# Sparse attention with a mixture of depths: transposes by 64-row halves, and a new order of the step

## The chip, the cores and the metric

The kernel runs on one core of a Trainium2 chip. A core has five engines that work side by side, each through its own queue in order: TensorE (matmuls, and transposes through it), VectorE, ScalarE, GpSimd and SyncE, which only issues DMAs here. They wait for each other through semaphores. The metric is the time of the device in microseconds for one execution, lower is better; three executions were timed. Cores and dies play no part, since there is only one core.

## The reference

Two blocks, one behind the other. Batch 8, 8 heads, 576 tokens, head size 64, all float32.

```python
scores = scale * np.matmul(q, k.transpose(0, 1, 3, 2))          # 8 x 8 x 576 x 576
kth = np.partition(scores, -top_k, axis=-1)[..., -top_k:-top_k + 1]   # top_k = 32
scores = np.where(scores >= kth, scores, -1e9)
attn = softmax(scores)
x = heads side by side of np.matmul(attn, v)                     # 8 x 576 x 512

for b in range(B):                                               # mixture of depths
    s = x[b] @ w_gate                                            # one gate for each token
    top = the 128 tokens of b with the largest gate
    h = np.maximum(x[b, top] @ w1, 0)                            # 512 -> 1024
    out[b] = x[b]
    out[b, top] += sigmoid(s[top])[:, None] * (h @ w2)           # 1024 -> 512
```

In each row of the scores only the 32 largest count. Finding the 32nd largest of each of 36,864 rows is the work that has no matmul in it.

## The kernel before, in words

**Units.** The work on the attention is cut into units of 128 query rows by two heads (the last 64 queries of a batch entry go as 64 rows by four heads). A batch entry has 18 units (4, 4, 4, 4 and 2), the kernel has N = 144. The list `units` holds them in order.

**Steps.** One long loop, `for n in range(-1, N)`, is a software pipeline written out by hand. In step n the engines work on six units at once:

- unit n + 1: TensorE multiplies queries by keys (`multiply`, into the four PSUM banks `ps`), ScalarE copies the scores to SBUF (`keep`, tile `sc`, of which there are five);
- unit n: VectorE searches the scores for a bound (`bound_of`): 14 instructions take the 8 largest of a seventh of a row for each of two heads (`cand`), then three rounds of maxima and replacements merge them (`best`, `bound`);
- unit n - 1: ScalarE takes the sign of bound minus score and counts it (`part`, tile `sides`, one instruction a head), GpSimd multiplies scores by signs (`y`, one product a head), so that what lies above the bound turns negative, and fills eight more places of `y` from the counts (`fill`);
- unit n - 2: VectorE takes the 8 largest of each row of `y` (`kth_of`, tile `next`); the last is the 32nd largest score;
- unit n - 3: the mask `less` of scores below the 32nd, in bfloat16, by ScalarE for the first head and by GpSimd for the second (`mask_of`);
- unit n - 4: TensorE turns the scores (`turn` for 4 chunks of each of two heads into the two banks `ptr`, `turn_last` for the rest of 64 + 64 columns into `av`), and on top of each transposed chunk it adds mask times -2^90 times the identity. ScalarE takes the exponential (`pT`, `last`), TensorE multiplies by the values into `av` (`values`), ScalarE copies the result (`xs`). The exponential of what is masked is 0; the sum of the weights comes from a column of ones beside the values.

**What rides along.** When a tile of 128 queries has all its heads, VectorE takes a reciprocal (`rden`) in the next step and GpSimd divides (`x`); one step later VectorE takes the dot product with the gate's weights (`prod`, in `dot`). It is placed in the middle of the search for candidates (`amid_late`), so it is queued between two of its instructions. When a batch entry is complete, its mixture of depths runs as a generator, `mixture`, of which the steps listed in `mix_at` call one piece each: counts of larger gates, a gather of 128 rows (an indirect DMA of GpSimd), four transposes (`xe_ps`), eight pieces of four matmuls (`h_ps`), eight matmuls (`y_ps`), a scatter that adds. In the step after a piece, `flush()` lets ScalarE copy what it left in PSUM. Keys and queries of the next batch entry are loaded by SyncE and turned in pieces (`loads`): TensorE puts up to two transposes into free columns of the scores' banks, and ScalarE copies them to `kT` or `qT`.

**What sets the order.** Every engine's instructions are kept in the order in which the program names them (`InOrder`, whose line 45 is therefore the line of nearly all instructions in the profile). So the order of calls in the loop is each engine's queue. In a step after the first ones, TensorE has: turn, last block, transposes of the loads, scores, values, the mixture's piece. ScalarE has: `pT`, `last`, `less`, copies left by the mixture in the step before, copies of the loads, `sc`, `xs`, and the two `sides`. GpSimd has: `less`, small work, two `y`, `fill`. VectorE has: candidates and merges for the bound, small work, two `next`. The first four steps have smaller banks and an order of their own. After step N - 1 an ending, written out, finishes the last units (`weigh_unit`, `values_unit`), the gates, and the mixtures of the last two batch entries.

Of the kernel before, what the change touches and what calls it, by code (L numbers as in the profile page):

```python
# [10 lines left out]
AF = mybir.ActivationFunctionType  # L11
ALU = mybir.AluOpType
FP32 = mybir.dt.float32
BF16 = mybir.dt.bfloat16
# [17 lines left out]
J = 4  # L32
# [16 lines left out]
def kernel(  # L49
# [12 lines left out]
    P = nc.NUM_PARTITIONS  # L62
# [4 lines left out]
    NT = J + 1  # L67
# [133 lines left out]
        )  # L201

    late, vector_late, pool_late = [], [], []
    amid_late = []

    kept, values_bank = [], [None]

    after_kth = []

    def flush():  # L210
        while late:
            late.pop(0)()

# [23 lines left out]
    class Rows:  # L237
# [370 lines left out]
    def turn_some(tr, z, less):  # L608

        pe.transpose(tr, z, ident)  # L610
        if less is not None:
            pe.matmul(
                tr, less, out_of_reach, start=False, stop=True, skip_group_check=True
            )

    def room_to_turn():
        return ps_tr.tile([P, 2, J, P], FP32, name="ptr"), ps_av.tile(
            [P, 512], FP32, name="av"
        )

    def turn(z, tr, less=None):

        for i in range(2):
            for c in range(J):
                at = slice(c * P + i * R, (c + 1) * P + i * R)
                turn_some(
                    tr[:, i, c, :], z[:, i, at], None if less is None else less[:, i, at]
                )

    def turn_last(z, av, less=None):  # L630

# [10 lines left out]
    def values(t, g, pT, last, av, vs):  # L642

        vt, vpair = vs  # L650
        for i, heads in enumerate(heads_of(t, g)):
            for c in range(J):
                for r in (0, R):
                    h = heads[-1 if r else 0][0]
                    pe.matmul(
                        av[r : r + R, i * DE : (i + 1) * DE],
                        pT[:, i, c, r : r + R],
                        vt[:, h, c, :],
                        start=(c == 0 and i == 0),
                        stop=False,  # L660
                        skip_group_check=True,
                    )
# [75 lines left out]
    def mixture(row0, pg, rank, exact=False):  # L738
# [116 lines left out]
        late.append(  # L855
            lambda ps=ps: act.copy(out=xeT, in_=ps.rearrange("p (c i) -> p c i", c=NDC))
        )
        hT = modpool.tile([P, NFC, CAP], FP32, name="hT")
        for fc in range(NFC):
            yield  # L860
            if fc == 1:
                vector_late.append(squash)
            if fc % 2 == 0:
                ps = ps_misc.tile([P, 2, CAP], FP32, name="h_ps", tag="misc")
            multiply_h(ps[:, fc % 2, :], fc, xeT)
            if fc % 2 == 1:
                late.append(
                    lambda ps=ps, fc=fc: act.activation(
                        hT[:, fc - 1 : fc + 1, :], ps, AF.Relu
                    )  # L870
                )

        for fc in range(NFC):
# [7 lines left out]
        late.append(  # L881
            lambda ps=ps: act.activation(gy, ps, AF.Copy, scale=g)
        )
        pool_late.append(lambda: add_rows(gy, row_i))

    def multiply_places(ps, pick, pg):

# [46 lines left out]
    def add_rows(gy, row_i):  # L934

        put_rows(gy, row_i, compute_op=ALU.add)
# [87 lines left out]
    for b in range(B - 1):  # L1024
        n = (b + 1) * per_batch + mix_at_of.get(b, mix_at)[6]
        mix_steps[n].remove(b)
        place_steps[n] = b
    mixtures = {}
    qkv = {0: room_for_qkv(0)}

# [15 lines left out]
    inverting = normalised = None  # L1046
    of_batch = {}
    scs, bounds, ys, next8s, masks = {}, {}, {}, {}, {}

    def is_unit(n):  # L1050
        return 0 <= n < N

    def weigh(sc, tr, av, less):

        turn(sc, tr, less)
        tr_last = turn_last(sc, av, less)
        pT = ptpool.tile([P, 2, J, P], FP32, name="pT")
        last = ptpool.tile([P, P], FP32, name="last")

        def exp():  # L1060
            act.activation(pT, tr, AF.Exp, scale=scale)
            act.activation(last, tr_last, AF.Exp, scale=scale)

        return pT, last, exp

    def bound_of(n):
        b, i = divmod(n, per_batch)
# [2 lines left out]
        find_bound(scs[n], bounds[b][:, i, :, :])  # L1070

    def what_is_below(n):
        at, sc = 2 * n, scs[n]
        b, i = divmod(n, per_batch)
        bound = bounds[b][:, i, :, :]
        sides = wkpool.tile([P, 2, S], BF16, name="sides")
        y = wkpool.tile([P, 2, S + 8], FP32, name="y")
        for i in range(2):
            part(i, sc, bound, at, sides)
            pool.tensor_tensor(y[:, i, 0:S], sc[:, i, :], sides[:, i, :], ALU.mult)  # L1080
        fill(y, at)
        ys[n] = y

    def kth_of(n):
# [23 lines left out]
    for n in range(-1, N):  # L1108
# [40 lines left out]

        if is_unit(n - 4):  # L1150
            tr, av = room_to_turn()
            pT, last, exp = weigh(scs.pop(n - 4), tr, av, masks.pop(n - 4))
            exp()
        if is_unit(n - 3):
            mask_of(n - 3, (act, None) if n in scatter_steps else None)
        flush()
        if is_unit(n + 1):
            b, t, g = units[n + 1]
            kT, qT = qkv[b][0:2]
            b, i = divmod(n, per_batch)  # L1160
            if n + 1 < NHP:
                ps = room_for_first_scores()
                multiply(t, g, kT, qT, ps)
                if is_unit(n - 1):
                    what_is_below(n - 1)
                stay_busy((10, 10, 20, 30)[n + 1])
            else:
                ps = room_for_scores()
                loads = list(islice(loading, first_loads[i] if b == 0 else loads_at[i]))
                halves = [ps[:, a, :, HALF : HALF + P] for a in range(2)]  # L1170
                for load, half in zip(loads, halves):
                    load[0](half)
                multiply(t, g, kT, qT, by_head(ps))
                for load, half in zip(loads, halves):
                    load[1](half)
                if n == NHP - 1:
                    stay_busy(20)
            scs[n + 1] = keep(ps)
        if is_unit(n - 4):
            b4, t4, g4 = units[n - 4]  # L1180
            values(t4, g4, pT, last, av, qkv[b4][2])
            if n in place_steps:
                values_bank[0] = av
                next(mixtures[place_steps[n]])
            if g4 == 0:
# [21 lines left out]
            after_kth.pop(0)()  # L1207


        if is_unit(n - 1) and n + 1 >= NHP:  # L1210
            what_is_below(n - 1)

        if gating is not None:
            b, t = gating
            if t == J:
                store(out[b], of_batch[b][0])
                mixtures[b] = mixture(float(b * S), of_batch[b][1], ranks[:, b, :])
        for b in mix_steps.get(n, ()):
# [21 lines left out]

    def weigh_unit(m):
        tr, av = other_room(m) if (N - m) % 2 else room_to_turn()
        weighed[m] = *weigh(scs.pop(m), tr, av, masks.pop(m)), av

    def values_unit(m):
        pT, last, _, av = weighed[m]
# [371 lines left out]
```

## Time and profile before

| | |
|---|---|
| median of three runs | 814.96 us (814.26 to 816.5) |
| the profiled execution | 816.28 us, of it the span of the profile 814.4 us |
| TensorE matmuls | 777.2 us busy, 10231 instructions |
| VectorE | 783.5 us busy, 4655 instructions |
| ScalarE | 729.5 us busy, 1577 instructions |
| GpSimd | 721.6 us busy, 722 instructions |
| DMA | 50.38 MB, mean 62 GB/s |
| TensorE's granted clock | 0.998 |

How to read it: the span is the time from the first to the last instruction in the trace, and the profiled execution takes 1.9 us more than its span. Busy is the time in which an engine has an instruction in work, waiting not included. A matmul's end is modelled and matmuls overlap each other, so TensorE's busy time says little; for it, the distance from one start to the next is the useful number. The same holds in a smaller way for VectorE and ScalarE: an instruction of `cand` lasts 0.227 us, but the next begins after 0.145 us.

Almost all is steady work. The first 40 us hold the loading of the first keys and queries, with VectorE 32.5 us busy. From 40 to 770 us a step takes 4.7 us at first and about 5.3 us on average once a mixture runs beside it; a batch entry takes 95.88 us (the exponential `pT` begins at 384.24 in one and at 480.12 in the same step of the next). The last 45 us are the ending, in which VectorE is 22.6 us busy.

The largest groups of the page's list of instructions:

```profile
L45 POOL TENSOR_TENSOR y<-sc,sides 128x576 f32<-128x576 f32 x288 | 365.8, 1294 | 51.0 <-ACT sides L45 49.3
L45 DVE MAX8 cand<-sc 128x8 f32<-128x82 f32 (+1 forms) x2016 | 314.0, 227 | 4.3 <-ACT sc L45 4.2
L45 POOL TENSOR_SCALAR less<-sc,next 128x576 bf16<-128x576 f32 x135 | 233.2, 1728 | 2.2 <-DVE next L45 1.2
L45 ACT ACTIVATE sides<-sc,bound 128x576 bf16<-128x576 f32 x288 | 223.5, 791 | 0.0
L45 PE MATMUL ptr<-out_of_reach,less 128*128 128x128 bf16 x1136 | 203.3, 219 | 18.0 <-POOL less L45 17.1
L45 PE MATMUL ptr<-ident,sc 128*128 128x128 f32 x1136 | 214.6, 280 | 0.0
L45 DVE MAX8 next<-y 128x8 f32<-128x584 f32 x288 | 204.4, 751 | 0.5 <-POOL y L45 0.5
L45 ACT ACTIVATE pT<-ptr 128x1024 f32<-128x1024 f32 x142 | 145.3, 1024 | 39.5 <-PE ptr L45 38.5
```

Each line gives engine and operation, tile written and tiles read, shapes, count, then busy us and mean ns of one, and last the idle time before them with what ended it. PE is TensorE, DVE VectorE, ACT ScalarE, POOL GpSimd, SP SyncE.

### The profile page before, as it was taken

The page shows a single profiled execution, that of the slowest core. Times are in us where ns is not written, and L with a number is a line of the kernel's source. Part 1 is how long each engine was busy: PE and PEld are TensorE (multiplying, and loading weights), DVE is VectorE, ACT ScalarE, POOL GpSimd, SP SyncE. Part 2 cuts the span into 40 slices and gives each one's busy share as a digit, 9 for nine tenths or more (in the row PEclk, how much of TensorE's full clock was granted, in tenths as well). Part 3 has the DMA queues.
Part 4 walks back from the last instruction along what each step waited for, and adds up shares of the span by engine and source line. Part 5 has one row for each costly group of instructions (what it writes and reads, how often), then busy time and mean ns, then how long its engine had stood idle before and what let it go on. Part 6 is the DMA issues. An engine that isn't in the chain of part 4 may idle for free. (4 is left out here: it accounts for less than half of the span.)

```text
span 814.4 us, 28453 instructions
## 1 busy us (share of the span) xinstructions
PE 777.2 (95%) x10231; PEld 600.3 (74%) x10231; DVE 783.5 (96%) x4655; ACT 729.5 (90%) x1577; POOL 721.6 (89%) x722
## 2 busy tenths in 40 slices
PE   8988888888999999999999999999999999999987
PEld 6766666667887778877787777877788777867756
DVE  6999999999999999999999999999999999999962
ACT  5999999999999999999999999999999999879840
POOL 3899999999999999999999999999999999998921
PEclk9999999999999999999999999999999999999999
DMA  8931214121151123221251221512224102001021
GB/s 169 287 89 28 52 58 106 29 53 28 60 114 26 43 59 90 66 54 33 74 106 29 54 41 60 100 28 54 41 80 94 28 3 79 23 5 25 2 72 30
DMA packets 121732, 50.38 MB, mean 62 GB/s; under 512 B 116016, under 2 KB 116016, under 8 KB 120560
## 3 DMA queue, kind: packets, MB, share of 16 engines
q1 hardware_dynamic: 118368, 43.94, 22.0%
q0 software_dynamic: 1744, 4.20, 2.9%
q8 instruction: 82, 1.34, 0.7%
q14 instruction: 66, 0.54, 0.2%
q10 hardware_dynamic: 1472, 0.36, 0.2%
HBM read 36.93 MB, written 11.55 MB: 60 GB/s over the span
## 5 line engine op out<-in xcount | busy, mean ns | idle before, releaser
L45 POOL TENSOR_TENSOR y<-sc,sides 128x576 f32<-128x576 f32 x288 | 365.8, 1294 | 51.0 <-ACT sides L45 49.3
L45 DVE MAX8 cand<-sc 128x8 f32<-128x82 f32 (+1 forms) x2016 | 314.0, 227 | 4.3 <-ACT sc L45 4.2
L45 POOL TENSOR_SCALAR less<-sc,next 128x576 bf16<-128x576 f32 x135 | 233.2, 1728 | 2.2 <-DVE next L45 1.2
L45 ACT ACTIVATE sides<-sc,bound 128x576 bf16<-128x576 f32 x288 | 223.5, 791 | 0.0
L45 PE MATMUL ptr<-out_of_reach,less 128*128 128x128 bf16 x1136 | 203.3, 219 | 18.0 <-POOL less L45 17.1
L45 PE MATMUL ptr<-ident,sc 128*128 128x128 f32 x1136 | 214.6, 280 | 0.0
L45 DVE MAX8 next<-y 128x8 f32<-128x584 f32 x288 | 204.4, 751 | 0.5 <-POOL y L45 0.5
L45 PEld LDWEIGHTS av<-v,pT 128*64 128x64 f32 x4608 | 146.1, 137 | 65.9 <-ACT last L45 62.6
L45 ACT ACTIVATE pT<-ptr 128x1024 f32<-128x1024 f32 x142 | 145.3, 1024 | 39.5 <-PE ptr L45 38.5
L45 PEld LDWEIGHTS ptr<-ident,sc 128*128 128x128 f32 x1136 | 159.9, 141 | 28.2 <-issue 16.7
L45 PE MATMUL ps<-kT,qT 64*128 64x288 f32 (+1 forms) x1248 | 174.0, 425 | 0.0
L45 PE MATMUL av<-v,pT 128*64 128x65 f32 x4608 | 166.0, 224 | 8.1 <-ACT last L45 7.4
L45 PEld LDWEIGHTS <-less 128*128 128x128 bf16 x1296 | 134.4, 104 | 36.7 <-POOL less L45 24.0
L45 ACT COPY sc<-ps 128x1152 f32<-128x1152 f32 x140 | 159.1, 1137 | 0.0
L45 PEld LDWEIGHTS ps<-kT,qT 64*128 64x128 f32 (+1 forms) x1248 | 95.8, 175 | 34.5 <-issue 20.9
L45 ACT ACTIVATE less<-sc,next 128x576 bf16<-128x576 f32 x141 | 109.8, 779 | 2.9 <-DVE next L45 2.8
L45 DVE MATCH_REPLACE8 cand<-best,cand 128x21 f32<-128x21 f32 (+1 forms) x576 | 98.9, 179 | 0.0
L45 DVE MAX8 best<-cand 128x8 f32<-128x21 f32 (+1 forms) x576 | 90.3, 189 | 0.0
L45 PE MATMUL h_ps<-xeT,w 128*128 128x128 f32 x464 | 65.7, 286 | 0.0
L45 PEld LDWEIGHTS h_ps<-xeT,w 128*128 128x128 f32 x464 | 55.8, 191 | 9.1 <-issue 7.0
L45 ACT ACTIVATION_READ_ACCUMULATOR sides<-sc,bound 128x1 f32 x288 | 61.0, 212 | 0.0
L45 PE MATMUL y_ps<-w,hT 128*128 128x512 f32 x112 | 60.6, 636 | 0.0
(165 smaller groups left out, 908.3 us busy)
## 6 DMA issues: line engine op xcount, KB each, us to landing
v<-in_v_dram SPq DMA_DIRECT2D x64, 128.0 KB, 4.4
out_dram<-x SPq DMA_DIRECT2D x8, 1024.0 KB, 4.0
rows<-in_k_dram SPq DMA_DIRECT2D x56, 128.0 KB, 2.9
rows<-in_q_dram SPq DMA_DIRECT2D x56, 128.0 KB, 3.0
w<-in_moe_w_dram SPq DMA_DIRECT2D x2, 2048.0 KB
gate_row<-row_dram SPq DMA_DIRECT2D x7, 288.0 KB, 4.4
last<-in_q_dram SPq DMA_DIRECT2D x8, 128.0 KB, 3.3
vpair<-in_v_dram SPq DMA_DIRECT2D x16, 64.0 KB, 3.9
```

Of the source, the lines that this page charges most:

```text
L45: return lambda *a, **kw: self._tc.keep_in_program_order(fn(*a, **kw))
```

## The change

It has four parts.

1. **Turning by halves.** A chunk of 128 rows by 128 columns is no longer transposed at once, but in two halves of 64 rows, one from partitions 0 to 63 and one from 64 to 127. (`by_half` is `a.rearrange("p r c (b i) -> p r (c b) i", i=64)`.) [...] The first half of all chunks goes to one bank of `ptr`, the second to the other, through the view `by_half`; `values` reads `pT` through the same view. The mask's matmul is halved in the same way. A turn has 16 + 16 matmuls in place of 8 + 8. `turn_last` stays whole.
2. **TensorE's order in a step.** Before: turn, last block, loads, scores, values, mixture. After: turn, scores, last block, loads, the mixture's piece, values. The mixture's first eight pieces (counts, places, the gather) stay where they were, behind the values.
3. **ScalarE's order in a step.** The first `sides` goes up behind `pT`, so ahead of `last` and `less`; the second stays, but ahead of `xs`. After: `pT`, `sides`, `last`, `less`, copies of the loads, `sc`, copies of the mixture, `sides`, `xs`.
4. **The mixture's copies** go to a list of their own, `copies_late`, which is emptied behind the scores' copy in the same step, where before they waited for the next step's `flush()`. The scatter of the result is still queued in the step after.

VectorE, GpSimd and SyncE have the same instructions in the same order as before. In the ending, `weigh_unit` turns by halves too, and calls the last block directly behind.

```diff
     def flush():
+        flush_copies()
         while late:
...
     def turn(z, tr, less=None):
+        to = by_half(tr)
+        halves = [slice(r * R, (r + 1) * R) for r in range(2)]
         for i in range(2):
             for c in range(J):
                 at = slice(c * P + i * R, (c + 1) * P + i * R)
-                turn_some(
-                    tr[:, i, c, :], z[:, i, at], None if less is None else less[:, i, at]
-                )
+                for r, q in enumerate(halves):
+                    pe.transpose(to[:, r, i * J + c, :], z[q, i, at], ident[q, q])
+                for r, q in enumerate(halves):
+                    if less is not None:
+                        pe.matmul(
+                            to[:, r, i * J + c, :], less[q, i, at], out_of_reach[q, q],
+                            start=False, stop=True, skip_group_check=True,
+                        )
...
-                        pT[:, i, c, r : r + R],
+                        by_half(pT)[:, r // R, i * J + c, :],
...
         if is_unit(n - 4):
             tr, av = room_to_turn()
-            pT, last, exp = weigh(scs.pop(n - 4), tr, av, masks.pop(n - 4))
+            pT, last, exp, turn_rest = weigh(scs.pop(n - 4), tr, av, masks.pop(n - 4))
             exp()
-        if is_unit(n - 3):
-            mask_of(n - 3, (act, None) if n in scatter_steps else None)
-        flush()
+        early = is_unit(n - 1) and n + 1 >= NHP
+        if early:
+            sign(n - 1, 0)
         if is_unit(n + 1):
...
                 ps = room_for_scores()
-                loads = list(islice(loading, ...))
-                halves = [ps[:, a, :, HALF : HALF + P] for a in range(2)]
-                for load, half in zip(loads, halves):
-                    load[0](half)
                 multiply(t, g, kT, qT, by_head(ps))
-                for load, half in zip(loads, halves):
-                    load[1](half)
+        if is_unit(n - 4):
+            turn_rest()()
+        if is_unit(n - 3):
+            mask_of(n - 3, (act, None) if n in scatter_steps else None)
+        flush()
+        if is_unit(n + 1) and n + 1 >= NHP:
+            loads = list(islice(loading, ...))
+            halves = [ps[:, a, :, HALF : HALF + P] for a in range(2)]
+            for load, half in zip(loads, halves):
+                load[0](half)
+            for load, half in zip(loads, halves):
+                load[1](half)
+        rest = []
+        for b in mix_steps.get(n, ()):
+            if pieces.get(b, 0) > PLACES:
+                next(mixtures[b], None)
+            else:
+                rest.append(b)
+            pieces[b] = pieces.get(b, 0) + 1
+        if is_unit(n + 1):
             scs[n + 1] = keep(ps)
+        flush_copies()
+        if early:
+            sign(n - 1, 1)
         if is_unit(n - 4):
             values(t4, g4, pT, last, av, qkv[b4][2])
...
-        if is_unit(n - 1) and n + 1 >= NHP:
-            what_is_below(n - 1)
+        if early:
+            weigh_signs(n - 1)
...
-        for b in mix_steps.get(n, ()):
+        for b in rest:
             next(mixtures[b], None)
```

`sign(n, i)` is the one `sides` instruction of head i, `weigh_signs(n)` the two products `y` and `fill`, which were together in `what_is_below`. In `mixture`, the three `late.append` of copies become `copies_late.append`.

More of the change, by code (lines that the diff above doesn't have):

```diff
@@ L203 @@
     late, vector_late, pool_late = [], [], []
+    copies_late = []
     amid_late = []
@@ L208, with flush_copies @@
     after_kth = []
+    def flush_copies():
+        while copies_late:
+            copies_late.pop(0)()
     def flush():
+        flush_copies()
         while late:
@@ L619, in room_to_turn, with by_half @@
         )
+    def by_half(a):
+        return a.rearrange("p r c (b i) -> p r (c b) i", i=R)
     def turn(z, tr, less=None):
+        to = by_half(tr)
+        halves = [slice(r * R, (r + 1) * R) for r in range(2)]
         for i in range(2):
@@ L625, in turn @@
                 at = slice(c * P + i * R, (c + 1) * P + i * R)
-                turn_some(
-                    tr[:, i, c, :], z[:, i, at], None if less is None else less[:, i, at]
-                )
+                for r, q in enumerate(halves):
[3 more added lines that the diff above has]
+                        pe.matmul(
+                            to[:, r, i * J + c, :],
+                            less[q, i, at],
+                            out_of_reach[q, q],
+                            start=False,
+                            stop=True,
+                            skip_group_check=True,
+                        )
     def turn_last(z, av, less=None):
@@ L854, in mixture @@
             )
-        late.append(
+        copies_late.append(
             lambda ps=ps: act.copy(out=xeT, in_=ps.rearrange("p (c i) -> p c i", c=NDC))
@@ L866, in mixture @@
             if fc % 2 == 1:
-                late.append(
+                copies_late.append(
                     lambda ps=ps, fc=fc: act.activation(
@@ L880, in mixture @@
         gy = modpool.tile([P, HD], FP32, name="gy")
[L881 to L884, printed above, removed]
+        copies_late.append(lambda: act.activation(gy, ps, AF.Copy, scale=g))
+        late.append(lambda: pool_late.append(lambda: add_rows(gy, row_i)))
     def multiply_places(ps, pick, pg):
@@ L1027 @@
         place_steps[n] = b
+    PLACES, pieces = NT + 2, {}
     mixtures = {}
@@ L1048 @@
     scs, bounds, ys, next8s, masks = {}, {}, {}, {}, {}
+    sides_of = {}
     def is_unit(n):
@@ L1055, in weigh @@
         turn(sc, tr, less)
-        tr_last = turn_last(sc, av, less)
         pT = ptpool.tile([P, 2, J, P], FP32, name="pT")
@@ L1061, in exp, with turn_rest @@
             act.activation(pT, tr, AF.Exp, scale=scale)
-            act.activation(last, tr_last, AF.Exp, scale=scale)
-        return pT, last, exp
+        def turn_rest():
+            tr_last = turn_last(sc, av, less)
+            return lambda: act.activation(last, tr_last, AF.Exp, scale=scale)
+        return pT, last, exp, turn_rest
     def bound_of(n):
@@ L1072, in what_is_below, with sign, weigh_signs @@
     def what_is_below(n):
[L1073 to L1076, printed above, removed]
+        for i in range(2):
+            sign(n, i)
+        weigh_signs(n)
+    def sign(n, i):
+        b, m = divmod(n, per_batch)
+        if i == 0:
+            sides_of[n] = wkpool.tile([P, 2, S], BF16, name="sides")
+        part(i, scs[n], bounds[b][:, m, :, :], 2 * n, sides_of[n])
+    def weigh_signs(n):
+        sc, sides = scs[n], sides_of.pop(n)
         y = wkpool.tile([P, 2, S + 8], FP32, name="y")
         for i in range(2):
-            part(i, sc, bound, at, sides)
             pool.tensor_tensor(y[:, i, 0:S], sc[:, i, :], sides[:, i, :], ALU.mult)
-        fill(y, at)
+        fill(y, 2 * n)
         ys[n] = y
@@ L1159 @@
             kT, qT = qkv[b][0:2]
-            b, i = divmod(n, per_batch)
             if n + 1 < NHP:
@@ L1168 @@
                 ps = room_for_scores()
-                loads = list(islice(loading, first_loads[i] if b == 0 else loads_at[i]))
-                halves = [ps[:, a, :, HALF : HALF + P] for a in range(2)]
-                for load, half in zip(loads, halves):
-                    load[0](half)
                 multiply(t, g, kT, qT, by_head(ps))
-                for load, half in zip(loads, halves):
-                    load[1](half)
-                if n == NHP - 1:
-                    stay_busy(20)
+        if is_unit(n - 4):
[4 more added lines that the diff above has]
+        if is_unit(n + 1) and n + 1 >= NHP:
+            b, i = divmod(n, per_batch)
+            loads = list(islice(loading, first_loads[i] if b == 0 else loads_at[i]))
+            halves = [ps[:, a, :, HALF : HALF + P] for a in range(2)]
[3 more added lines that the diff above has]
+                load[1](half)
+            if n == NHP - 1:
+                stay_busy(20)
+        rest = []
[6 more added lines that the diff above has]
+        if is_unit(n + 1):
             scs[n + 1] = keep(ps)
+        flush_copies()
+        if early:
+            sign(n - 1, 1)
         if is_unit(n - 4):
@@ L1184 @@
                 next(mixtures[place_steps[n]])
+                pieces[place_steps[n]] += 1
             if g4 == 0:
@@ L1242, in weigh_unit, with both @@
         tr, av = other_room(m) if (N - m) % 2 else room_to_turn()
-        weighed[m] = *weigh(scs.pop(m), tr, av, masks.pop(m)), av
+        pT, last, exp, turn_rest = weigh(scs.pop(m), tr, av, masks.pop(m))
+        exp_rest = turn_rest()
+        def both():
+            exp()
+            exp_rest()
+        weighed[m] = pT, last, both, av
     def values_unit(m):
```

## The prediction

> **What bounds the kernel now.** I read busy time by stages first, to see which engine has no room; then the waits of that engine; then the waits of the others; then one instruction whose time is not its own. Columns of the first view: stretch in us, its length, busy us (instructions) of TensorE, its weight loads, VectorE, ScalarE, GpSimd.
>
> ```profile
> 40.00:770.00 730.00, 704.68 (x9494) 544.10 (x9488) 728.54 (x4364) 685.93 (x1478) 685.89 (x658) 1.00 0.23 54
> ```
>
> ```profile
> DVE next L45 <- POOL y L45: 0.3, 1, 0.3
> ```
>
> The second line is the whole list of VectorE's waits from 40 to 770 us: one wait of 0.3 us. VectorE is busy 728.5 of 730 us there, 90% of the span, and that is real work: in the steps without extras the search for candidates begins at 26.88, 31.61, 36.35 and 41.10 us, 4.74 us apart, with nothing idle between. So no wait of another engine that the change removes can shorten this stretch, unless a VectorE instruction itself gets shorter. The other engines' waits from 200 to 700 us:
>
> ```profile
> PEld av L45 <- ACT last L45: 40.6, 89, 1.1
> ACT pT L45 <- PE ptr L45: 23.0, 62, 0.7
> POOL y L45 <- ACT sides L45: 22.4, 41, 1.2
> ```
>
> This is what the change is built on: TensorE stands before the values, ScalarE before its large exponential, GpSimd before a product. All three sit behind a full VectorE. One VectorE instruction, though, has no fixed length: the gate's dot product (`prod`, two tensors in), min/median/max in ns:
>
> ```profile
> L45 DVE CUSTOM_DVE_ANT_0 prod<-x,wg x40: 677/954/1966, 52.4 to 784.4; 128x512 f32<-128x512 f32 x32, 64x512 f32<-64x512 f32 x8
> ```
>
> Two of them, with what GpSimd did beside them (start, duration):
>
> ```profile
> 399.62 2.52 POOL L45 TENSOR_TENSOR y<-sc,sides 128x576 f32<-128x576 f32 x2
> ...
> 401.27 1.42 DVE L45 CUSTOM_DVE_ANT_0 prod<-x,wg 128x512 f32<-128x512 f32 x1
> ...
> 402.10 0.67 POOL L45 TENSOR_TENSOR y<-steps,seen 128x16 f32<-128x16 f32 x1
> ...
> 402.75 1.72 POOL L45 TENSOR_SCALAR less<-sc,next 128x576 bf16<-128x576 f32 x1
> ```
>
> ```profile
> 190.14 0.68 DVE L45 CUSTOM_DVE_ANT_0 prod<-x,wg 128x512 f32<-128x512 f32 x1
> ```
>
> ```profile
> 189.38 1.73 POOL L45 TENSOR_SCALAR less<-sc,next 128x576 bf16<-128x576 f32 x1
> ```
>
> At 401.27 the second product `y` is running until 402.14; the dot takes 0.87 us of waiting and then 0.55. At 190.14 `less` has been running for 0.76 us and the dot takes its 0.68. Those that begin 0.46 and 0.34 us after a `less` (168.58, 147.21) take 0.82 and 0.95: `less` is in the way for its first 0.6 us only, a `y` to its end. From 40 to 770 us the 38 dots take 40.86 us; at 0.68 each they would take 25.8. **That 15.0 us is all the change can win in the VectorE-bound stretch.**
>
> [...] the score matmuls alternate between partitions 0 to 63 and 64 to 127, and a pair of 288 f32 columns takes 0.243 us, while full-height f32 matmuls of 128 columns follow each other by 0.112, which is 0.25 for a single one of 288. [...] I use start-to-start distances.
>
> **The change part by part.**
>
> Turning by halves. Now one chunk is an f32 transpose (0.115 to the next start) and the mask's bf16 matmul (0.056), 0.171; eight are 1.37 us. After, it is two transposes and two mask matmuls, each 64 rows high and 64 columns wide[...]. Upper bound: none overlap. A 64-row transpose of the last queries follows the one before by 0.061 (four from 399.93), and a half-wide mask matmul costs no more than today's 0.056: 2 x 0.061 + 2 x 0.056 = 0.234, a turn 1.87 (+0.50). Lower bound: both pairs overlap and the mask costs half: 0.061 + 0.028 = 0.089, a turn 0.71 (-0.66). I take 0.85, near the lower end, because the scores do overlap; the loads of 16 more pairs of weights are what I add. TensorE's waits from 200 to 700 us for `last` are 44.5 us over 94 steps, 0.47 a step, so even the upper end just fits its slack.
>
> Scores before the last block, loads and mixture before the values. These move TensorE's work into the wait for `last`; no instruction is added or dropped. Worth 0.47 us a step to TensorE, nothing to the end by itself. No DMA is issued by the moved parts except that the refill of the loads' rows (SP) follows its transposes some 1 us later in the step; its data is used more than one step later. The mixture's copies (hidden layer, gathered rows, result) now run in the step of their products instead of the next; they are the same instructions, 0.27 to 0.57 us each, and the scatter that the last one feeds is still queued a step later, so they cost nothing while ScalarE has its slack (below), and up to 0.27 us of delay for the second `sides` in the steps that have one.
>
> ScalarE's order. One step now (start, duration):
>
> ```profile
> 405.58 1.02 ACT L45 ACTIVATE pT<-ptr 128x1024 f32<-128x1024 f32 x1
> 406.50 0.27 ACT L45 ACTIVATE last<-av 128x128 f32<-128x128 f32 x1
> 406.66 0.78 ACT L45 ACTIVATE less<-sc,next 128x576 bf16<-128x576 f32 x1
> ...
> 407.84 1.15 ACT L45 COPY sc<-ps 128x1152 f32<-128x1152 f32 x1
> ...
> 409.01 0.82 ACT L45 ACTIVATE sides<-sc,bound 128x576 bf16<-128x576 f32 x1
> ...
> 409.78 0.81 ACT L45 ACTIVATE sides<-sc,bound 128x576 bf16<-128x576 f32 x1
> ```
>
> After: pT 0.92, first sides 0.77, last 0.16, less 0.67, a load's copy 0.26, sc 1.00, the mixture's copy, second sides 0.77, xs 0.16: the same 4.71 us of start-to-start times, with `less` 0.77 later (at pT + 1.85) and the scores' copy done at pT + 3.9 (now + 3.4). Without the 23 us of waiting for `ptr`, ScalarE needs about 18 x 4.71 + 4 (the mixture's copies, sums, second loads) = 89 us a batch, where VectorE needs 95.88 (pT at 384.24 and 480.12). So ScalarE, TensorE and GpSimd run ahead until ScalarE's `less` waits for VectorE's `next`. That sets the phase: VectorE's step starts (S) up to 1.75 us after pT, where now it is between -0.5 and +0.7.
>
> The dots in the new phase. GpSimd's `less` waits for the `next` that ends at S + 0.1. The step before a dot always has the division `x`. From S + 0.1: less 1.69, x 1.00, two y 2.48, padding 0.19 (start-to-start, 396.93 on and 189.19 on) is 5.36, so GpSimd is free at S + 5.46. VectorE's step with its reciprocal is 4.85, so this is S' + 0.61, where the next `less` starts. The dot starts at S' + 1.30 (401.27 against 399.97). It meets a `less` that has run for 0.69 us: free, 0.68. Allowing 0.1 for GpSimd's other small work I take 0.78. Bounds: 0.68, and 1.42 if GpSimd is later and the dot meets the second `y`. The first two dots (52.40, 73.10: 1.75 and 1.27) come before the lead has built up and are left as they are: 3.02 + 36 x 0.78 = 31.1 against 40.86: **-9.8 us**.
>
> Start. In step 3 the scores' copy goes behind a first `sides`: it ends at 26.55 + 0.77 = 27.3, while VectorE wants it at 26.88: **+0.5 us**, once. In later steps the copy is ready 0.2 us or more ahead (31.87 against 32.08).
>
> End. The last turn begins when VectorE has its mask (777.98) and ScalarE's exponential waits for it; a turn shorter by 0.5 passes through: **-0.5 us**.
>
> Sum: -9.8 + 0.5 - 0.5 = -9.8 us. The profiled execution (span 814.4, 816.28 in all) would have a span of 804.6; taken from the runs' median of 814.96 this is 805.2. When the dots are free VectorE is late by nothing else: what is next is its own 4.74 us a step.
>
> **The rivals.**
> - The dots keep their length, because GpSimd (686 of 730 us busy) stays where it is relative to VectorE. For it: its work alone is near a step. Against: 22.4 us of its waits are for `sides`, half of which come 2.6 us earlier. Start and end cancel: 815.0.
> - Slower, through the dots: GpSimd ends its second `y` later than S' + 1.3, because that product waits for the second `sides`, which is now behind the scores' copy and the mixture's. It decides once GpSimd is 0.7 us later than worked out above. Then each dot is like the one at 401.27: 36 x 1.42 + 3.0 = 54.1, +13.3 + 0.5 - 0.5: 828.
> - Slower, through TensorE: halves neither overlap nor hide their loads, a turn costs over 1.87 us and TensorE takes VectorE's place. At 0.2 us a step over 125 steps: 840. Against it: the score pairs above.
> - The dots become free from the first one on: -15.0, 800.
>
> **How the numbers follow.** Forecast 0.62 (its own range 800 to 812), dots unchanged 0.15, dots longer 0.15, TensorE 0.04, all dots free 0.04. Range 800 to 816: the two slower rivals (0.19) are left out above, nothing below 800 is reachable but for the tail. A difference of 0.3% (2.4 us) is about what a measurement of this kernel tells from none. Of "dots unchanged" a third would still be over 2.4 us: faster 0.62 + 0.04 + 0.05 = 0.71, same 0.10, slower 0.19.
>
> **What would show it.** Right: VectorE over 99.5% busy from 40 to 770 us with no new wait; `prod` with a median near 0.75 us; ScalarE's `less` waiting for `next`; no wait of ScalarE for `ptr` over 5 us; starts of chunks in a turn near 0.1 us apart. Wrong: VectorE waiting for `sc` or `y` in mid-kernel, a `prod` median over 1 us, or TensorE's weight loads busy without gaps.

## The result, and the profile after

The changed kernel takes 802.86 us (median of four runs, 802.82 to 803.03), the kernel before 814.62 beside it: a ratio of 0.9851, 95% interval 0.9834 to 0.9868. That is 11.8 us less, where 9.8 were forecast (805.2, range 800 to 816). The profiled span goes from 814.4 to 800.5 us.

First the busy time by stages, as before (stretch, length, busy us of TensorE, weight loads, VectorE, ScalarE, GpSimd, then clock):

```profile
40.00:770.00 730.00, 670.69 (x11935) 506.40 (x11932) 726.07 (x4386) 692.15 (x1497) 674.06 (x662) 1.00 0.23 55
```

VectorE has no more room than before, yet it runs 4386 instructions in this stretch instead of 4364: each step is shorter. VectorE's whole list of waits there is one line:

```profile
DVE rden L45 <- ACT sums L45: 1.4, 1, 1.4
```

So the time came out of VectorE instructions. The group of the gate's dots (min/median/max in ns), by tile:

```profile
L45 DVE CUSTOM_DVE_ANT_0 prod<-x,wg x40: 668/680/1596, 50.3 to 771.0; 128x512 f32<-128x512 f32 x32, 64x512 f32<-64x512 f32 x8
```

The median falls from 954 to 680 ns, and the 40 dots from 42.23 to 30.49 us: 11.74 us. Two of them on the timeline, with GpSimd beside them (start, duration):

```profile
372.35 1.72 POOL L45 TENSOR_SCALAR less<-sc,next 128x576 bf16<-128x576 f32 x1
...
373.13 0.68 DVE L45 CUSTOM_DVE_ANT_0 prod<-x,wg 128x512 f32<-128x512 f32 x1
```

```profile
403.71 1.72 POOL L45 TENSOR_SCALAR less<-sc,next 128x576 bf16<-128x576 f32 x1
...
404.17 0.82 DVE L45 CUSTOM_DVE_ANT_0 prod<-x,wg 64x512 f32<-64x512 f32 x1
```

From the third dot to the last before the ending, every dot now begins 0.46 to 0.48, 0.71 to 0.78 or 1.00 to 1.03 us after a `less` and meets no product `y` until its own last 0.02 us. The ones at 0.46 still lose 0.14 us (0.82 against 0.68) to the end of the first 0.6 us of `less`. What sets that phase is in the waits from 200 to 700 us:

```profile
PEld av L45 <- ACT last L45: 48.6, 59, 1.1
...
POOL less L45 <- DVE next L45: 26.9, 48, 1.0
...
ACT sides L45 <- DVE bound L45: 9.5, 21, 0.6
ACT pT L45 <- PE ptr L45: 5.9, 14, 0.7
```

GpSimd and ScalarE now wait for VectorE's results (`next`, `bound`); in the kernel before, that list had ScalarE waiting 23.0 us for the turn and GpSimd 22.4 us for `sides`, and none for `next` or `bound`. That was a sign, in the trace before, that VectorE did not set the pace alone there: with VectorE as the only limit, the others would have had to wait for its results.

The span's 13.95 us, by parts: VectorE's first candidates begin 1.58 us earlier (9.22 and 7.63 us), from there to the last `next` of the loop 12.66 us less (11.74 of it dots, 0.72 VectorE's idle gaps), and the ending 0.29 us more. The first of these is not the change: in the other executions below the same point falls between 7.7 and 9.2 us in either form of the kernel, and the profiled execution of the kernel before was 1.7 us above the median of its runs.

### The profile page after: what moved, and what is told of

Read it like the earlier page. It is cut to its first block, busy times and chain, and to the rows that moved or that the text cites. A ratio compares the mean times of both kernels' runs of the same rounds, so it can differ in the third digit from the quotient of the medians.

```text
span 800.5 us, 33285 instructions
## 1 busy us (share of the span) xinstructions
PE 728.1 (91%) x12535; PEld 550.2 (69%) x12535; DVE 771.6 (96%) x4655; ACT 728.4 (91%) x1577; POOL 706.4 (88%) x722
## 5 line engine op out<-in xcount | busy, mean ns | idle before, releaser
L45 POOL TENSOR_TENSOR y<-sc,sides 128x576 f32<-128x576 f32 x288 | 366.9, 1304 | 17.7 <-ACT sides L45 16.6
L45 ACT ACTIVATE sides<-sc,bound 128x576 bf16<-128x576 f32 x288 | 229.6, 797 | 17.0 <-DVE bound L45 13.1
L45 PEld LDWEIGHTS <-less 64*128 64x128 bf16 (+1 forms) x2448 | 157.6, 129 | 29.3 <-POOL less L45 24.6
L45 PE MATMUL ps<-kT,qT 64*128 64x288 f32 (+1 forms) x1248 | 170.1, 422 | 0.3 <-ACT sc L45 0.3
L45 PE MATMUL ptr<-out_of_reach,less 64*128 64x64 bf16 x2272 | 151.0, 190 | 17.3 <-POOL less L45 16.6
L45 PE MATMUL ptr<-ident,sc 64*128 64x64 f32 x2272 | 166.3, 252 | 0.0
L45 PEld LDWEIGHTS ptr<-ident,sc 64*128 64x128 f32 x2272 | 138.6, 137 | 23.8 <-issue 21.2
L45 PEld LDWEIGHTS ps<-kT,qT 64*128 64x128 f32 (+1 forms) x1248 | 92.8, 176 | 17.6 <-ACT sc L45 0.4
L45 PE MATMUL h_ps<-xeT,w 128*128 128x128 f32 x464 | 61.9, 278 | 0.0
L45 PEld LDWEIGHTS av<-ident,sc 128*128 128x128 f32 x144 | 20.0, 139 | 54.8 <-issue 44.9
L45 PE MATMUL av<-vpair,last 128*64 128x130 f32 x576 | 56.9, 276 | 0.0
```

Source lines behind the costliest of these rows:

```text
L45: return lambda *a, **kw: self._tc.keep_in_program_order(fn(*a, **kw))
```

## Experiments

Two theories stood against each other after this result. The first (theory A in the expectations, the rival where work is added to the kernel before), the prediction's, is that VectorE alone sets the pace of both kernels and the gain is its dots getting out of GpSimd's way. The second (theory B, later the two-limits theory) is that the kernel before was also held by a loop through the other engines (turn, exponential and signs, products, mask, next turn), and that a dot which waits only shows that loop's time on VectorE. All kernels ran beside the kernel before (814.5 to 815.5 us).

**The dot moved out of the way, in both kernels.** The dot goes behind the whole search for the bound; all else stays.

```diff
-                if (i, u) == (1, 2) and amid_late:
-                    amid_late.pop()()
...
+        if amid_late:
+            amid_late.pop()()
```

> The kernel before, with one edit: the gate's dot product is queued behind the whole search for the bound instead of in its middle, about 2.1 us later in VectorE's step. Theory A [...]: GpSimd's mask less, which begins about 0.65 us after the dot's old place, has then run for over 1.2 us, so dots are near 0.68 us; 38 of them go from 40.9 to about 26 to 28 us and the time falls to 800 to 803 us, with nothing of the change in it. Theory B (the gain comes from shorter steps of TensorE and ScalarE): the time stays at 814 to 816 us.

> The changed kernel with the same edit: the dot product behind the whole search. In the new phase GpSimd's less starts with VectorE's step and is over after 1.8 to 2.5 us, so at 3.4 us a product y is running. Theory A: dots of 1.2 us or more on average, 38 x 0.5 or more added: 815 to 830 us, the gain gone though every other part of the change is still there. Theory B: the time stays at 803 us.

In the kernel before: 816.53 us, ratio 1.0024 (1.0014 to 1.0035), where the first theory gave 800 to 803. Its dots did fall, from 42.23 to 37.27 us, but a batch entry still took 95.9 us from one `next` to that of the same step in the next entry. VectorE's list of waits from 40 to 740 us shows where the 5 us went:

```profile
DVE next L45 <- POOL y L45: 2.4, 7, 0.4
```

With the short gaps besides, VectorE's idle time from the first candidates to the last `next` grew by 4.8 us (2.81 to 7.58), all of it ahead of `next` and 2.1 us of it in one wait of the last steps, at 772.9: what the dots gave up came back as waiting for the products. In the changed kernel: 832.81 us, ratio 1.0209 (1.0188 to 1.0229), somewhat above the first theory's 815 to 830 and far from the second's 803.

```profile
L45 DVE CUSTOM_DVE_ANT_0 prod<-x,wg x40: 672/1380/3320, 52.4 to 801.9; 128x512 f32<-128x512 f32 x32, 64x512 f32<-64x512 f32 x8
```

The late dot meets the products again. The dots took 61.22 us, 30.7 more than in the changed kernel, and the span grew by 30.9. So in the changed kernel a dot's waiting is paid in full; in the kernel before, less of it bought nothing. The first theory held for the second kernel and missed for the first.

**Halves alone, and orders alone.** The first keeps the old orders and turns by halves (with the layout of the values' reads); the second has all the new orders with whole transposes.

```diff
 # halves alone: kernel before, with
+    to = by_half(tr)
+    for r, q in enumerate(halves):
+        pe.transpose(to[:, r, i * J + c, :], z[q, i, at], ident[q, q])
...
+                        by_half(pT)[:, r // R, i * J + c, :],
 # orders alone: changed kernel, with
+    turn_some(tr[:, i, c, :], z[:, i, at], None if less is None else less[:, i, at])
...
+                        pT[:, i, c, r : r + R],
```

> The kernel before with the turn by halves alone (and the values reading the new layout); all orders as before. A turn takes 0.94 us in place of 1.37. Theory B: most of the gain, 803 to 806 us. Theory A: the time is 814.6 plus what the dots differ from 42.2 us in sum; GpSimd still gets both sides late in ScalarE's step, so its less begins some 0.9 us after VectorE's step and the dots are near 0.9 to 1.0: 811 to 815 us, with VectorE as full as before.

> The changed kernel with whole transposes as before (1.37 us a turn), all new orders kept. Theory A: the early first sides lets GpSimd run up to VectorE, dots near 0.75 us in median, 802 to 807 us. Theory B (the quicker turn makes it): 812 us or more, with ScalarE waiting for ptr.

Halves alone: 808.76 us, ratio 0.994 (0.9916 to 0.9964), half of the gain, and between the ranges of the two theories. Its steady batch entries (those in the middle, which all take the same time) take 94.47 us, as long as the changed kernel's 94.56 and 1.4 less than before (95.89). What is missing lies at the start: its first ten dots take 13.0 us, where the changed kernel's take 8.7, and the other thirty 22.6 against 21.8. These two differences are 5.2 us; the spans differ by 5.3.

Orders alone: 820.33 us, ratio 1.007 (1.0052 to 1.0089), slower than the kernel before. That is a miss for the first theory (802 to 807) and within what the second gave (812 or more, with ScalarE waiting for `ptr`). Waits from 200 to 700 us:

```profile
PEld av L45 <- ACT pT L45: 32.1, 82, 0.4
ACT pT L45 <- PE ptr L45: 32.0, 62, 0.9
POOL y L45 <- ACT sides L45: 29.8, 46, 1.3
PEld av L45 <- ACT last L45: 26.2, 40, 0.8
```

As these waits read: with the values last in TensorE's step, the next turn comes later by what they waited, ScalarE waits for that turn, and GpSimd for ScalarE. A steady batch entry takes 97.5 us. VectorE's own waits are back too (4.4 us for `found`, 2.3 for `sc`, from 40 to 740).

**More work for VectorE.** If VectorE sets the pace, work added to it is paid in full. Behind each dot of the search, one maximum is taken three times instead of once.

```diff
+                times = 1
                 if (i, u) == (1, 2) and amid_late:
                     amid_late.pop()()
+                    times = 3
-                dve.max(
+                for _ in range(times):
+                    dve.max(
```

> The kernel before with two more 82-column maxima of VectorE behind each dot of the middle search (each repeats the one beside it; 0.145 us from start to start, so 0.29 us x 38 dots = 11.0 us of VectorE work). Two-limits theory (before, VectorE and the loop turn, exponential, products, turn set the pace together, and part of each dot's length is only the loop's time seen on VectorE): the dots take up nothing new and the loop hides most of the work, +0 to +4 us, 815 to 819. Rival (VectorE alone sets the pace of the kernel before, as predicted): all of the added work is paid, +11 us, about 826; and if the dots also move out of the products' way, a little less, 822 to 826.

> The changed kernel with the same added work, 11.0 us of VectorE. Two-limits theory: VectorE alone sets the pace of the changed kernel, +10 to +12 us, 813 to 815, and the dots stay near 0.7 us. Rival (the changed kernel is bound by TensorE or the loop as well): under +6 us, below 809.

> Halves alone (808.8) with the same two repeated maxima behind each dot as in the two runs with added work (22 us of VectorE by what those showed: 0.28 us each, since a repeat onto the same output starts only when the one before it has ended). Two-limits theory: with that much work VectorE sets the pace in every one of these kernels, so it ends where the kernel before and the changed kernel with the same work ended, 824.8 to 826.4, and a steady batch entry takes 97.4 us against 94.47 (all of 5 x 0.57 us). Rival (halves alone is still held by the loop in its steady batches): a steady batch under 96.5 us, in all 820 to 823.

The size was wrong: a repeat begins 0.28 us after the one before it, when that has ended (the maxima there last 0.23 to 0.25 us): in the program it waits for a semaphore that the one before raises, as the maxima beside it do not. In the changed kernel's trace the three begin 0.28, 0.28 and 0.16 us apart, where one took 0.145: 0.58 us a dot, 22.0 us over 38 dots.

The changed kernel: 824.85 us, ratio 1.0117 (1.0094 to 1.014), +22.0 on 802.86. All of it is paid. The kernel before: 826.36 us, ratio 1.0142 (1.0119 to 1.0165), +11.8 on 814.6, just over half. Most of the other half is seen in its dots, which fell by 8.9 us, to 33.37:

```profile
L45 DVE CUSTOM_DVE_ANT_0 prod<-x,wg x40: 670/695/1749, 50.5 to 794.2; 128x512 f32<-128x512 f32 x32, 64x512 f32<-64x512 f32 x8
```

And ScalarE and GpSimd now wait for VectorE's `next`, which they did not do from 200 to 700 us in the kernel before:

```profile
ACT less L45 <- DVE next L45: 17.2, 35, 0.9
POOL less L45 <- DVE next L45: 16.7, 28, 1.1
```

Read by their size as expected (+11.8 where the rival said +11), these numbers would speak for the rival; with the work that was really added they speak for two limits. A steady batch entry says it most plainly: 95.89 to 97.57 us in the kernel before, 94.56 to 97.38 in the changed one. With VectorE this full the two kernels are 0.2 us apart per entry, without the added work 1.3. So the kernel before had some 10 us of room on VectorE that its busy time did not show, because it lay inside waiting dots.

With halves alone: 831.07 us, ratio 1.0186 (1.0163 to 1.0208). The steady entry came out as expected (97.62, from 94.47), the total did not: 6.6 us of span above the changed kernel with the same work, of which 6.5 are its dots (36.83 against 30.30), again mostly the first ten. More VectorE work does not repair the phase at the start; the orders do.

**Each order by itself.** Halves and old orders with only the new places of the two `sides` (the first early, the second ahead of `xs`); the changed kernel without the early `sides`; the changed kernel with the mixture's copies a step later.

```diff
 # early sides alone (halves, TensorE and copies as before; the second ahead of xs)
             exp()
+        early = is_unit(n - 1) and n + 1 >= NHP
+        if early:
+            sign(n - 1, 0)
+        if is_unit(n - 4):
+            exp_last()
...
             scs[n + 1] = keep(ps)
+        if early:
+            sign(n - 1, 1)
 # late sides (changed kernel)
-            sign(n - 1, 0)
...
-            sign(n - 1, 1)
...
-            weigh_signs(n - 1)
+            what_is_below(n - 1)
 # late copies (changed kernel)
-        copies_late.append(
+        late.append(
```

> Turning by halves with TensorE's order, the loads and the mixture's copies as before; of the new orders only ScalarE's early first sides. Two-limits theory: the early sides lets GpSimd begin its products earlier, it runs up to VectorE's next already in the first batch entries, and the dots there shrink as in the changed kernel: 803 to 806. Rival (what the orders add comes from TensorE filling its wait for last): the early sides alone brings nothing beyond halves alone, 808 to 810.

> The changed kernel with both sides at the late place of the kernel before, behind the values; halves, TensorE's order and the copies' place stay. Halves alone measured 808.8, the whole change 802.9. If TensorE's order (scores ahead of the last block and of the values, so that the wait for last is filled) makes the rest of the gain: 802 to 804.5. If the early sides is needed for GpSimd to run up to VectorE in the first batch entries: 807 to 810, with dots of 1.0 us and more there.

> The changed kernel with the copies of the mixture's products back in the next step's flush, ahead of the scores' copy. If they only ride along (same instructions, ScalarE has slack): 802 to 804. If their place matters, because they stand ahead of the scores' copy and of the second sides or because the mixture's next products wait for their bank: 805 to 812, with VectorE waiting for sc or GpSimd for sides in the batches with a mixture.

None came out as expected; all are slower than the kernel before. Early `sides` alone: 836.59 us, ratio 1.0259 (1.0234 to 1.0283). Its waits from 200 to 700 us:

```profile
PEld av L45 <- ACT last L45: 69.9, 90, 1.1
ACT pT L45 <- PE ptr L45: 42.8, 76, 1.2
```

With halves alone these two were 43.8 and 7.7 us. As they read, the early `sides` puts `last` 0.77 us later, TensorE has nothing to fill the longer wait with, so the next turn is late and ScalarE waits for it. Late `sides`: 818.14 us, ratio 1.0044 (1.0029 to 1.006).

```profile
PEld L45 <- POOL less L45: 36.3, 71, 1.0
...
POOL y L45 <- ACT sides L45: 25.7, 46, 2.0
```

Here the turn waits 36 us for GpSimd's `less`, against 16.7 in the changed kernel: `sides` stands behind `xs`, which waits for values that are now TensorE's last work of the step, so the products start late. Late copies: 843.63 us, ratio 1.0358 (1.0342 to 1.0374).

```profile
PEld h_ps L45 <- ACT hT L45: 25.4, 15, 1.7
...
PEld h_ps L45 <- ACT xeT L45: 14.1, 6, 2.5
...
DVE cand L45 <- ACT sc L45: 10.7, 20, 1.4
```

The mixture's piece now stands ahead of the values, and if its copy (`hT`, `xeT`) waits for the next step's flush, the next piece holds up the values behind it. VectorE then waits for scores. So the parts carry each other. That they do is measured; how is read from the waits: the early `sides` needs the scores in the wait for `last`, that order needs the early `sides`, and the mixture's new place needs its copies at once.

**A later dot, and a TensorE kept busy.** Two improvements on the changed kernel: the dot two candidates (0.29 us) further on; and, with that, 30 matmuls of a constant ahead of the ending's turn that waits.

```diff
-                if (i, u) == (1, 2) and amid_late:
+                if (i, u) == (1, 4) and amid_late:
...
     def weigh_unit(m):
         tr, av = other_room(m) if (N - m) % 2 else room_to_turn()
+        if m == N - 3:
+            for _ in range(30):
+                pe.matmul(tr[:, 0, 0, :], out_of_reach, out_of_reach)
```

> The changed kernel with the dot two candidates later in the middle search (0.29 us). If a less of GpSimd is in the way for its first 0.6 us only: the dots that begin 0.46 us after a less (0.82 us each) begin 0.75 us after it and take 0.68; the ones at 0.78 and 1.03 stay free. 25 or so dots x 0.14 = -2 to -3 us: 800 to 801.5. Rival (the dots keep their 0.76 on average because the phase of less follows): 802.5 to 803.5.

> The changed kernel with the dot two candidates later and, in the ending, 30 matmuls of a constant (written over by the turn that follows) ahead of the turn that waits 1.95 us for VectorE's less. If the granted clock of 0.61 behind that wait is what lengthened the ending: clock 1.00 there, ending 0.5 to 0.9 us shorter than in the changed kernel (37.2 to 37.6 from the last next of the steps' loop to the end), in all 799.7 to 800.3. If the clock falls for another cause, or the ending is not TensorE's: the ending stays at 38.1, in all 800.8.

The later dot: 800.75 us, ratio 0.9826 (0.9805 to 0.9847), as expected. The dots take 27.96 us, 2.53 less, and the span is 2.6 less:

```profile
L45 DVE CUSTOM_DVE_ANT_0 prod<-x,wg x40: 661/673/1335, 50.5 to 768.3; 128x512 f32<-128x512 f32 x32, 64x512 f32<-64x512 f32 x8
```

The second is about the ending, which in the changed kernel grew by 0.29 us (37.83 to 38.12, from the loop's last `next` to the end). The changed kernel's timeline of TensorE, and its busy time by stages there:

```profile
757.54 0.20 PE L45 MATMUL tr<-out_of_reach,less 64*128 64x64 bf16 x2 [1.95 <-DVE less L45]
```

```profile
757.50:761.50 4.00, 3.87 (x66) 3.29 (x68) 4.00 (x9) 2.15 (x5) 2.13 (x3) 0.61 0.00 0
```

The third number from the right is the granted clock: 0.61 after the wait of 1.95 us. With the 30 matmuls, which fill 1.84 us of it, the same stage reads:

```profile
755.20:759.20 4.00, 3.91 (x101) 3.20 (x101) 4.00 (x9) 2.35 (x6) 2.08 (x3) 1.00 0.01 4
```

The ending falls to 36.87 us. With the later dot alone it was 38.16, so the busy wait is worth 1.3 us where at most 0.9 was expected; the granted clock of the whole profiled execution was 0.997 without the matmuls and 1.000 with them. The kernel falls to 798.89 us, ratio 0.9807 (0.9794 to 0.9821), below the 799.7 expected at the least. Of the 1.86 us between the two medians 1.3 are the ending; the rest is within the spread of the later dot's own four times (799.81 to 801.59). That is the fastest of all, 1.9% below the kernel before.

## Why the prediction was right, and where not

- **VectorE as the bound, and the dots as the only elastic part.** Right for what the change could win and how: 11.74 us of the span are dots. Incomplete for the kernel before. "VectorE is busy 728.5 of 730 us there, ... and that is real work" was the weak step: some of it was dots waiting, and the runs with late dots and with more work showed that another limit, 95.9 us a batch entry, lay as close, and set the pace. Free dots alone were expected to bring the kernel before to 800 to 803 us; with 5 us less of dots it took 1.7 more. The prediction's argument on the phase did not depend on this step: it had ScalarE held back by its waits for `ptr`, which is a wait inside that loop, and running ahead without them. So what was right was not luck, but the reason for 95.88 us was another than stated.
- **Turning by halves: 0.85 us taken, bounds 0.71 and 1.87.** From 200 to 700 us the two halves of a chunk begin 3 ns apart in the median (0 to 16), so they run side by side. A chunk takes 0.118 us (0.090 from transposes to mask, 0.028 on to the next chunk), eight of them 0.94 us, against 1.37 before. The mask's pair cost the assumed 0.028, the transposes 0.090 instead of 0.061. TensorE is not the bound, so this hid itself. One sum was off: the 44.5 us of waits for `last` add the matmuls' 3.9 to the weight loads' 40.6, and these are the same waits. That leaves 0.43 us a step, and the upper bound of +0.50 would not have fitted.
- **New orders "worth ... nothing to the end by itself".** As a set they were worth about 6 us: 808.76 with halves alone, 802.86 with all. The incomplete sets of orders that were run cost time: 818 to 844 us. The step that priced moved work at nothing because the instructions are the same held only with all parts present.
- **What locks the phase.** Forecast: ScalarE's `less` waits for `next`. Seen: GpSimd's `less` waits for it, 26.9 us, and ScalarE's first `sides` for `bound`, 9.5 us. ScalarE needs the first head's `next`, which begins 0.67 us before the second's. The effect on the dots is as worked out, because their phase was computed from GpSimd's `less`: 0.69 us into it was forecast, 0.46 to 1.03 was measured.
- **The dots: -9.8 us forecast, -11.74 measured, the term that was mis-sized.** The first two, left at 3.02 us, took 2.60; the other 36, put at 0.78, took 0.74 on average (26.5 us), as most are entirely free.
- **Start: +0.5 us.** The wait for `sc` in step 3 came, with 0.31 us at 25.17, and one of 0.59 at 11.73. But the kernel before had waited 1.1 us at its own start, beside the 3.1 us before its first candidates, so nothing was lost. From the first candidates to step 4 they take 17.7 us before and 17.5 after.
- **End: -0.5 us.** This failed: +0.29. A quicker turn arrives earlier at the same `less` of VectorE, and behind its wait of 1.95 us the granted clock fell (0.61 over the next 4 us). With the clock kept, the ending is 0.96 us shorter than before, and with halves alone, where the clock stayed at 1.00, 0.78 shorter. The misses at the start (about -0.5 us) and at the end (+0.8) nearly cancel in the sum, and that is luck.
- **What it gave as signs.** VectorE over 99.5% busy without a new wait: 99.46%, with a new one of 1.4 us. Median of `prod` near 0.75: 0.68. ScalarE's wait for `ptr` at most 5 us: 5.9. Starts of chunks near 0.1 us apart: 0.118. The first and the third were narrowly missed. Of the signs of being wrong none came.

What stays open: which link of the loop held the kernel before at 95.9 us. Halves shorten the turn and the limit goes, so the turn is in it; no run lengthened or shortened ScalarE's or GpSimd's link alone. Why the new orders, as a set, free the first ten dots is not shown either, only that they do.

## What to carry over

An engine that is 99.8% busy can still have room, when one of its instructions waits within its own time and the waiting counts as work (in the kernel before a dot took as little as 0.68 us beside no product and up to 1.97 beside two; busy time leaves out waits between instructions, not a wait inside one): compare that instruction's longest and shortest times, and add known work to see whether it is paid. Price a set of moves as a set: in a queue in order, each move is bought by the gap that another one opens, and half of a good change can be worse than none. And after TensorE is made quicker, look at what it waits for next, since the clock can fall there: here it was 0.61 over the 4 us behind a wait of 1.95 us.

## What had not been expected of the hardware

- **A dot can wait through two products.** In the kernel before with the late dot, from its timeline:

```profile
189.36 3.37 DVE L45 CUSTOM_DVE_ANT_0 prod<-x,wg 128x512 f32<-128x512 f32 x1
...
189.64 2.52 POOL L45 TENSOR_TENSOR y<-sc,sides 128x576 f32<-128x576 f32 x2
```

  The dot began 0.28 us before the first product, while GpSimd's gather was still running (188.43 to 189.62 us), and ended 0.57 us after the second. That is not always so: in the kernel before, the dot at 73.10 us also began beside a first product, ended 0.55 us after it, and the second product took 1.72 us instead of 1.28. What decides between the two is open. The measurement that stands: a dot of 0.68 us can take 3.4.
- **Around a wait of 1.95 us the clock fell.** In the changed kernel's ending the granted clock was still 1.00 when the matmuls began again (757.54 us), fell to 0.50 some 0.9 us later, and stayed there for 3.4 us; 30 matmuls of a constant in that wait kept it at 1.00. In the same execution it stayed at 1.00 behind a wait of 1.53 us, which ended at 721.65 us. Whether the length of the wait decides is not shown.
- **A repeated maximum cost 0.28 us** from start to start instead of 0.145. In the program each of the two repeats waits for a semaphore that the maximum before it raises; in the trace it begins after that one's end, as the maxima there last 0.229 to 0.250 us. What two such maxima would take without that semaphore was not run.
